# A new front, a shifted block order and a second load of v in an attention and MoE kernel

## The chip, the cores and the metric

The kernel runs on one core of a Trainium2 chip. The metric is the device time of one execution in microseconds (us); lower is better. A profile comes from one profiled execution, and its span runs from the first to the last instruction of that execution.

## The reference

Shapes: q, k, v are `[8, 8, 576, 64]` (batch, head, token, width) in float32; the two weights are `[512, 2048]` and `[2048, 512]`.

```
q_d, k_d, v_d = means over groups of 4 tokens           # 144 coarse tokens
out_d     = softmax(q_d k_d^T / 8) v_d                  # full attention, coarse
out_local = softmax(q k^T / 8 where |i - j| < 4) v      # a band of 7 keys for each query
attn      = repeat(out_d, 4 times along the tokens) + out_local
x   = attn, heads side by side: [4608, 512]
out = elu(x @ w_in) @ w_out                             # [4608, 512], float32
```

## The kernel before

The work falls into two parts. Attention goes by batch (8 of them) and, in a batch, by pairs of heads (j = 0 to 3). The two matrix products go by blocks of 512 tokens (t = 0 to 8). A batch has 576 tokens, so block t needs batch t and, from block 1 on, the end of the batch before it.

**One pair of heads.** `load` brings q as fp16 (a casting DMA of GpSimd's queue) and k, v as fp32 (SP's queue). Queries are cut into 6 blocks of 96 tokens, so each partition gets 12 runs of 256 bytes; k and v have 6 more partitions, filled by small DMAs, for the 3 neighbours on each side. `cast` turns k and v to fp16 on GpSimd. `transposes` multiplies q and k by constant matrices (QI, KI), which gives in one pass the transposed rows and their means over 4, and does the same for v's means with VR (L172); ScalarE and VectorE evict the results (qt, kt, kd, vd). `scores` makes the band's scores (L200) and the coarse scores (L210), ScalarE takes the exponentials (L218, L222), and VectorE multiplies by a 0/1 mask (L228).

**One batch.** `denominators` sums the exponentials of all four pairs by matmuls with an indicator (IND) and VectorE takes the reciprocal. The reciprocals are spread over the partitions: for batch 0 by matmuls (`spread_pe`), for the others through DRAM, by DMAs that ScalarE's queue issues (`spread_out`, `spread_in`). `outputs` makes the weighted sums of v (L321, L327), VectorE multiplies by the reciprocals (gn, ln), and GpSimd adds the two parts into xt, the input of the first product (L348).

**One block.** `mm1(t, fc)`, fc = 0 to 15, is 4 matmuls of 128x512 (L364), an exponential on ScalarE (L369), and two steps on VectorE (L370, L373) that give elu. `mm2(t, i)`, i = 0 to 15, is again 4 matmuls (L384); four such steps make 128 tokens of the output, which ScalarE copies and SP stores. So a block costs 32 groups of 4 matmuls. "Group" means such four matmuls below.

**Order.** Nothing is reordered at run time: every step is an event with a time on an abstract scale, the events are sorted, and each engine gets its instructions in that order. One unit of that scale is one `mm1` and, where there is one, one `mm2`. In the kernel before:

```
def start_of(t):
    return 0 if t == 0 else 16 * (t + 1)
...
at(start_of(t) + s + 0.25, mm1, t, s)
at((16 if t == 0 else start_of(t + 1)) + s + 0.75, mm2, t, s)
```

So all of batch 0's attention comes first, then mm1 of block 0 alone (with batch 1 among it), mm2 of block 0 alone, mm1 of block 1 alone (with batch 2), and from then on mm1 of block t beside mm2 of block t - 1, with batch t + 1 among them. The last two blocks have no attention beside them. "Stage t" means mm1 of block t and what stands beside it.

PSUM has 8 banks: two double banks (tag `two`) for all of attention, two banks `hp` for mm1, two `misc` for mm2, the denominators and half of the early mm1.

Of the kernel before, what the change touches and what calls it, by code (L numbers as in the profile page):

```python
# [9 lines left out]
FP16 = mybir.dt.float16  # L10
FP32 = mybir.dt.float32
AB = mybir.AluOpType
AF = mybir.ActivationFunctionType

# [3 lines left out]
QB, KW, NB = 96, 102, 6  # L18
HB = 3 * QB
QW, KWW = QB + 24, 24 + KW  # L20
DM, DFF, NTOK = 512, 2048, 4608
TBLK = 512
# [3 lines left out]
RW = S + SD  # L26
KG = SD // 2


def _np_consts():  # L30

    off = np.concatenate([np.arange(96), np.arange(-3, 0), np.arange(96, 99)])
    m = np.zeros((KW, NB, QB), dtype=np.float16)
    for c in range(NB):
        for u in range(QB):
            ok = (np.abs(off - u) < 4) & (off + QB * c >= 0) & (off + QB * c < S)
            m[ok, c, u] = 1.0
    r = np.zeros((KW, 24), dtype=np.float16)
    r[np.arange(96), np.arange(96) // 4] = 0.25
    qi = np.concatenate([np.eye(96, dtype=np.float16), r[:96]], axis=1)  # L40
    ki = np.concatenate([r, np.eye(KW, dtype=np.float16)], axis=1)
    vr = np.zeros((KW, 120), dtype=np.float16)
    vr[:, 48:72] = r
    indl = np.zeros((128, 37), dtype=np.float16)
    indl[:, 5] = 1.0
    seed = np.zeros((2, 32 + HB), dtype=np.float16)
    seed[0, 6:32] = 1.0
    seed[1, 4:6] = 1.0
    seed[0, 32:] = 1.0
    seed[1, 32 + SD :] = 1.0  # L50
    sel = np.zeros((NPAIR, 32, 3, 2, 64), dtype=np.float16)
    for e in range(2):
        for g in range(2):
            sel[:, 2 * e + g, g, e] = 1.0
        sel[:, 4 + e, 2, e] = 1.0
    return m, qi, ki, vr, indl, seed, sel.reshape(128, 384)
# [12 lines left out]
def kernel(  # L69
# [11 lines left out]
    ps = ctx.enter_context(tc.tile_pool(name="ps", bufs=1, space=bass.MemoryType.PSUM))  # L81
    dr = ctx.enter_context(tc.tile_pool(name="dr", bufs=1, space=bass.MemoryType.DRAM))
    ctx.enter_context(nc.allow_low_precision("fp16 operands of TensorE"))

    def const(a, name):
        t = sb.tile(list(a.shape), FP16, tag=name, bufs=1, name=name)
        nc.sync.dma_start(out=t[:], in_=nc.inline_tensor(a, name=name + "c").ap())
        return t

    def two(name):  # L90
        return ps.tile([128, 2, 512], FP32, tag="two", bufs=2, name=name)

    m_np, qi_np, ki_np, vr_np, ind_np, seed_np, sel_np = _np_consts()
    QI, KI = const(qi_np, "QI"), const(ki_np, "KI")
    consts = {}

    def late_consts():
        consts["VR"] = const(vr_np, "VR")
        consts["MASK"] = const(m_np, "MASK")
        consts["IND"] = const(ind_np, "IND")  # L100
        consts["SEED"] = const(seed_np, "SEED")
        consts["SEL"] = const(sel_np, "SEL")

    WI = sb.tile([128, DMC, DFF], FP16, tag="WI", bufs=1, name="WI")
    WO = sb.tile([128, FCN, DM], FP16, tag="WO", bufs=1, name="WO")

    def load_weights(i):

        if i < 8:
            src = moe_w_in.rearrange("(c p) m -> p c m", p=128)[:, :, 256 * i : 256 * i + 256]  # L110
            to = WI[:, :, 256 * i : 256 * i + 256]
        else:
            n = 2 * (i - 8)
            src = moe_w_out.rearrange("(c p) m -> p c m", p=128)[:, n : n + 2, :]
            to = WO[:, n : n + 2, :]
        nc.gpsimd.dma_start(out=to, in_=src)


    st16, stT, stB, stS, stR = {}, {}, {}, {}, {}

    st32 = {}

    def load(b, j):
        q16 = sb.tile([QB, 2, NB, 64], FP16, tag="q16", bufs=5, name="q16")
        k32 = sb.tile([KW, 2, NB, 64], FP32, tag="k32", bufs=3, name="k32")
        v32 = sb.tile([KW, 2, NB, 64], FP32, tag="v32", bufs=3, name="v32")

        def rows(src, c0, nblk, tok, n):
            a = src[b, 2 * j]
            blocks = [[QB * D, 2 * NB]] if nblk == NB else [[S * D, 2], [QB * D, nblk]]  # L130
            return bass.AP(
                tensor=a.tensor, offset=a.offset + (QB * c0 + tok) * D,
                ap=[[D, n], *blocks, [1, D]],
            )

        nc.gpsimd.dma_start(out=q16[:], in_=rows(q, 0, NB, 0, QB))  # L136
        for src, dst in ((k, k32), (v, v32)):
            nc.sync.dma_start(out=dst[0:96], in_=rows(src, 0, NB, 0, QB))
            lo = 1 if (b, j) == (0, 0) else 0
            hi = NB - 1 if (b, j) == (B - 1, NPAIR - 1) else NB  # L140
            if lo or hi < NB:
                nc.gpsimd.memset(dst[96:KW, :, 0 if lo else NB - 1, :], 0.0)
            for c0, nblk, tok, p in ((lo, NB - lo, -3, 96), (0, hi, QB, 99)):
                to, a = dst[p : p + 3, :, c0 : c0 + nblk, :], rows(src, c0, nblk, tok, 3)
                if nblk == NB:
                    nc.sync.dma_start(out=to, in_=a)
                else:
                    for e in range(2):
                        nc.sync.dma_start(out=to[:, e], in_=a[:, e])
        st32[(b, j)] = (q16, k32, v32)  # L150

    def cast(b, j):
        q16, k32, v32 = st32.pop((b, j))
        k16 = sb.tile([KW, NB, 2, 64], FP16, tag="k16", bufs=2, name="k16")
        v16 = sb.tile([KW, NB, 2, 64], FP16, tag="v16", bufs=8, name="v16")
        nc.gpsimd.tensor_copy(out=k16[:], in_=k32[:].rearrange("p e c d -> p c e d"))  # L156
        nc.gpsimd.tensor_copy(out=v16[:], in_=v32[:].rearrange("p e c d -> p c e d"))  # L157
        st16[(b, j)] = (q16, k16, v16)


    def transposes(b, j):
        q16, k16, v16 = st16.pop((b, j))
        VR = consts["VR"]
        tq, tk = two("tq"), two("tk")
        for c in range(NB):
            for e in range(2):
                nc.tensor.matmul(  # L167
                    tq[64 * e : 64 * e + 64, c // 3, QW * (c % 3) : QW * (c % 3) + QW],
                    q16[:, e, c, :], QI[:], start=True, stop=True,
                )  # L170
        for c in range(NB):
            nc.tensor.matmul(  # L172
                tq[0:KG, c // 3, 3 * QW : 3 * QW + 128],
                VR[:, 48 - 24 * (c % 3) : 120 - 24 * (c % 3)], v16[:, c, :, :],
                start=(c % 3 == 0), stop=(c % 3 == 2),
            )
        qt = sb.tile([128, 2, 3 * QW], FP16, tag="qt", bufs=2, name="qt")
        nc.scalar.copy(out=qt[:], in_=tq[:, :, 0 : 3 * QW])  # L178
        vd = sb.tile([KG, 2, 128], FP16, tag="vd", bufs=8, name="vd")
        nc.vector.tensor_copy(out=vd[:], in_=tq[0:KG, :, 3 * QW : 3 * QW + 128])  # L180
        for c in range(NB):
            nc.tensor.matmul(  # L182
                tk[:, c // 3, KWW * (c % 3) : KWW * (c % 3) + KWW], k16[:, c, :, :], KI[:],
                start=True, stop=True,
            )
        tk4 = tk[:, :, 0 : 3 * KWW].rearrange("p g (c w) -> p g c w", w=KWW)
        kt = sb.tile([128, 2, 3, KW], FP16, tag="kt", bufs=2, name="kt")
        nc.scalar.copy(out=kt[:], in_=tk4[:, :, :, 24:KWW])  # L188
        kd = sb.tile([128, 2, 3, 24], FP16, tag="kd", bufs=2, name="kd")
        nc.vector.tensor_copy(out=kd[:], in_=tk4[:, :, :, 0:24])  # L190
        stT[(b, j)] = (qt, kt, kd, vd, v16)


    def scores(b, j):
        qt, kt, kd, vd, v16 = stT.pop((b, j))
        sc = [two("sc"), two("sc")]
        for c in range(NB):
            for e in range(2):
                r = slice(64 * e, 64 * e + 64)
                nc.tensor.matmul(  # L200
                    sc[e][0:KW, c // 3, QB * (c % 3) : QB * (c % 3) + QB],
                    kt[r, c // 3, c % 3, :],
                    qt[r, c // 3, QW * (c % 3) : QW * (c % 3) + QB],
                    start=True, stop=True,
                )
        for kg in range(2):
            for e in range(2):
                r = slice(64 * e, 64 * e + 64)
                qd = _free(qt[r, 0, QB : QB + 1], [[QW, NB], [1, 24]])
                nc.tensor.matmul(  # L210
                    sc[e][0:KG, kg, HB : HB + SD],
                    _free(kd[r, 0, 0, 0:1], [[1, SD]])[:, KG * kg : KG * kg + KG], qd,
                    start=True, stop=True,
                )
        pex = sb.tile([KW, 2, S], FP16, tag="pex", bufs=2, name="pex")
# [272 lines left out]
```

## Time and profile before

| | us |
|---|---|
| three runs | 399.96, 401.83, 402.24 (median 401.83) |
| span of the profiled execution | 396.9 |
| first matmul of mm1 (block 0) | 46.40 after the start |
| end of the last mm2 matmul | 392.96 after the start |
| TensorE busy | 354.1 (89% of the span) |
| VectorE busy | 244.8 (62%) |
| ScalarE busy | 203.8 (51%) |
| GpSimd busy | 136.6 (34%) |

The profiled execution's own device time is not given apart from its span. The median of the three runs is 4.9 us above that span, and this 4.9 us is taken as what lies around a span. PE is TensorE, DVE is VectorE, ACT is ScalarE, POOL is GpSimd. In a timeline a row gives the start, the time from the first to the last of the merged instructions, the engine, the line, what is written from what, and in brackets the idle time before it with what ended it.

### The profile page before, as it was taken

Reading aid. Unit: us, or ns where it says so; the run is one execution under the profiler, and the core shown is the slowest. Engines: PE = TensorE matmul, PEld = TensorE weight load, DVE = VectorE, ACT = ScalarE, POOL = GpSimd, SP = SyncE. Lnnn points to the kernel's source line nnn. Section 1 sums busy time; section 2 is a strip of 40 time slices with the busy share of each in tenths; the row PEclk is TensorE's granted clock in tenths of the full one; section 3 lists DMA queues with packets and bytes.
Section 4 is the critical chain, followed back from the end, with each engine's and each line's share of the span. In section 5 each row is a group of like instructions: output and inputs, shape, how many; then the busy total and the mean of one; then the engine's idle time right before and its main releaser. Section 6 shows DMA issues by size and latency. Waiting matters only on the chain.

```text
span 396.9 us, 8379 instructions
## 1 busy us (share of the span) xinstructions
PE 354.1 (89%) x3244; PEld 183.9 (46%) x3244; DVE 244.8 (62%) x460; ACT 203.8 (51%) x377; POOL 136.6 (34%) x184
## 2 busy tenths in 40 slices
PE   0465699996987899999999999999999899999995
PEld 0343344553544455545555554555544444444442
DVE  0123578643697976877697769766977575555510
ACT  1363158643675475657556664666375334444421
POOL 4375694402930860383038204800520040000000
PEclk9999999998998999999999999999999999999999
DMA  9899999728996892997399439906401400101112
GB/s 125 154 187 176 182 191 183 106 25 167 202 125 146 168 85 55 206 196 48 79 229 168 31 96 226 168 2 138 122 26 36 129 28 26 54 26 38 43 53 80
DMA packets 138083, 44.91 MB, mean 113 GB/s; under 512 B 122580, under 2 KB 133436, under 8 KB 138044
## 3 DMA queue, kind: packets, MB, share of 16 engines
q1 hardware_dynamic: 85644, 29.79, 31.9%
q0 software_dynamic: 43776, 8.92, 25.9%
q10 hardware_dynamic: 8624, 5.68, 6.5%
q8 instruction: 25, 0.41, 0.5%
q14 instruction: 14, 0.11, 0.1%
HBM read 43.33 MB, written 9.95 MB: 134 GB/s over the span
## 4 chain that ended last, share of the span: by engine, by line
PE 77%; DVE 6%; ACT 5%; DMA 4%; ACTq 2%; issue 2%; POOL 1%; SPq 1%; POOLq 0%; DVEq 0%
PE op L384 30%; PE hp L364 28%; PE sc L200 4%; PE tq L172 3%; PE tq L167 3%; DMA v<-in_v_dram 3%; PE lg L321 3%; DVE gt L373 2%; ACTq L272 2%; PE tk L182 2%; ACT pex L218 2%; DVE e L370 1%; DMA rd<-rc 1%; DVE mex L228 1%; POOL xt L348 1%
## 5 line engine op out<-in xcount | busy, mean ns | idle before, releaser
L364 PE MATMUL hp<-xt,WI 128*128 128x512 f16 x576 | 150.1, 388 | 2.5 <-POOL xt L348 1.4
L384 PE MATMUL op<-WO,gt 128*128 128x512 f16 x576 | 145.8, 382 | 0.0
L369 ACT ACTIVATE e<-hp 128x512 f16<-128x512 f32 x144 | 85.6, 601 | 106.2 <-PE hp L364 96.3
L373 DVE SCALAR_TENSOR_TENSOR gt<-hp,e 128x512 f16<-128x512 f32 x144 | 99.6, 692 | 5.4
L370 DVE TENSOR_SCALAR e<-e 128x512 f16<-128x512 f16 x144 | 55.9, 388 | 53.1 <-ACT e L369 52.0
L364 PEld LDWEIGHTS <-WI 128*128 128x128 f16 x576 | 54.4, 99 | 68.4 <-issue 9.3
L384 PEld LDWEIGHTS <-gt 128*128 128x128 f16 x576 | 54.4, 98 | 63.5 <-issue 1.8
L156 POOL CAST k<-k 102x768 f16<-102x768 f32 x32 | 26.8, 836 | 95.1 <-DMA k<-in_k_dram 54.0
L348 POOL TENSOR_TENSOR xt<-ln,gn 128x512 f16<-128x512 f16 (+7 forms) x64 | 42.1, 689 | 46.9 <-DVE ln L339 46.9
L218 ACT ACTIVATE pex<-sc 102x576 f16<-102x576 f32 x64 | 41.4, 647 | 21.8 <-PE sc L210 21.6
L228 DVE TENSOR_TENSOR mex<-pex,MASK 102x1152 f16<-102x1152 f16 x32 | 26.2, 817 | 38.6 <-ACT pex L218 38.4
L157 POOL CAST v<-v 102x768 f16<-102x768 f32 x32 | 29.7, 927 | 37.3 <-DMA v<-in_v_dram 37.2
L178 ACT CAST qt<-tq 128x720 f16<-128x720 f32 x32 | 24.3, 758 | 35.3 <-PE tq L172 31.2
L390 ACT COPY os<-op 128x512 f32<-128x512 f32 x36 | 21.2, 588 | 19.9 <-PE op L384 19.9
L200 PE MATMUL sc<-qt,kt 64*102 64x96 f16 x384 | 18.9, 224 | 12.9 <-ACT kt L188 7.2
L180 DVE CAST vd<-tq 72x256 f16<-72x256 f32 x32 | 13.4, 417 | 27.5 <-ACT qt L178 26.5
L136 POOL DMA_DIRECT2D q<-in_q_dram x32 | 28.6, 893 | 3.9 <-DMA WI<-in_moe_w_in_dram 3.0
L167 PE MATMUL tq<-QI,q 96*64 96x120 f16 x384 | 17.4, 230 | 10.4 <-DMA q<-in_q_dram 5.9
L200 PEld LDWEIGHTS <-kt 64*102 64x102 f16 x384 | 14.0, 132 | 27.1 <-ACT kt L188 13.2
L222 ACT ACTIVATE dex<-sc 72x288 f16<-72x288 f32 x64 | 25.8, 404 | 0.0
L172 PE MATMUL tq<-v,VR 102*72 102x128 f16 x192 | 18.0, 234 | 7.0 <-POOL v L157 7.0
L339 DVE TENSOR_TENSOR ln<-lg,rcb 128x576 f16<-128x576 f32 x32 | 23.9, 746 | 0.0
(35 smaller groups left out, 211.9 us busy)
## 6 DMA issues: line engine op xcount, KB each, us to landing
k<-in_k_dram SPq DMA_DIRECT2D x32, 288.0 KB
v<-in_v_dram SPq DMA_DIRECT2D x32, 288.0 KB
out_dram<-os SPq DMA_DIRECT2D x36, 256.0 KB
q<-in_q_dram POOLq DMA_DIRECT2D x32, 144.0 KB, 4.5
rcb<-rd ACTq DMA_DIRECT2D x14, 288.0 KB
WI<-in_moe_w_in_dram POOLq DMA_DIRECT2D x8, 256.0 KB, 10.8
WO<-in_moe_w_out_dram POOLq DMA_DIRECT2D x8, 256.0 KB, 9.3
rcb<-rd ACTq DMA_DIRECT2D x14, 72.0 KB
```

Of the source, the lines that this page charges most:

```text
L157: nc.gpsimd.tensor_copy(out=v16[:], in_=v32[:].rearrange("p e c d -> p c e d"))
L167: nc.tensor.matmul(tq[64 * e : 64 * e + 64, c // 3, QW * (c % 3) : QW * (c % 3) + QW], q16[:, e, c, :], QI[:], start=True, stop=True,)
L172: nc.tensor.matmul(tq[0:KG, c // 3, 3 * QW : 3 * QW + 128], VR[:, 48 - 24 * (c % 3) : 120 - 24 * (c % 3)], v16[:, c, :, :], start=(c % 3 = ...
L200: nc.tensor.matmul(sc[e][0:KW, c // 3, QB * (c % 3) : QB * (c % 3) + QB], kt[r, c // 3, c % 3, :], qt[r, c // 3, QW * (c % 3) : QW * (c % ...
L218: nc.scalar.activation(out=pex[:, e, :].rearrange("p (g u) -> p g u", g=2), in_=sc[e][0:KW, :, 0:HB], func=AF.Exp, scale=SCALE,)
L228: nc.vector.tensor_tensor(out=mex[:], in0=pex[:], in1=mk2, op=AB.mult)
L348: nc.gpsimd.tensor_tensor(out=xt(t)[:, j, t0 - TBLK * t : t1 - TBLK * t], in0=ln[:, a:z], in1=_rep4(gn[:, a // 4 : z // 4]), op=AB.add,)
L364: nc.tensor.matmul(hp[:], WI[:, dc, 128 * fc : 128 * fc + 128], x[:, dc, :], start=(dc == 0), stop=(dc == DMC - 1),)
L369: nc.scalar.activation(out=e[:], in_=hp[:], func=AF.Exp)
L370: nc.vector.tensor_scalar(out=e[:], in0=e[:], scalar1=1.0, scalar2=-1.0, op0=AB.min, op1=AB.add)
L373: nc.vector.scalar_tensor_tensor(out=gts[t][:, fc, :], in0=hp[:], scalar=0.0, op0=AB.max, in1=e[:], op1=AB.add)
L384: nc.tensor.matmul(op_[:], gts[t][:, fc, 128 * tt : 128 * tt + 128], WO[:, fc, :], start=(fc == 0), stop=(fc == FCN - 1),)
```

## The change

In words:

- **Front.** q and k of batches 0 and 1 come as fp16 through GpSimd's queue in runs of 1536 bytes (6 tokens in a row on each of 96 partitions), transposed by TensorE's transpose (into fp16 PSUM) and put in order by the eviction. The sums over 4 tokens are taken from the transposed rows: by VectorE in batch 0, by GpSimd in batch 1. The band's mask is added by a matmul (`masked_scores`) before the exponential, so batches 0 and 1 need no multiplication by the mask. 14 matmuls of zeros run first and 2 more after the first pair. PSUM is split otherwise while batch 0 runs (three double banks, two single ones). The order of batch 0 is written out pair by pair (`first_batch`).
- **Constants** are loaded through ScalarE's queue. The weights come in larger pieces: w_in between the loads of batch 1, w_out within stage 0.
- **Order.** `start_of(t)` is 16 t: mm1 of block 1 runs beside mm2 of block 0. Four of the 16 steps of `mm2(0, i)` come at the end of stage 0.
- **Spreading.** Batches 0 to 2 spread the reciprocals by matmuls (one pair at a time); the others through DRAM as before, but SP's queue issues the DMAs.
- **Later batches.** q of batches 2 to 7 comes as fp32 by SP's queue and is cast by GpSimd; its transposing takes 6 matmuls per pair instead of 12. k has no extra partitions: the neighbours come from a padded transposed row (KT). v has 8 extra rows on each side within one DMA.
- **Sums of v.** Batches 3 to 7 load v a second time (`load_groups`, runs of 1024 bytes), and GpSimd adds the four tokens (`group_v`); the matmuls with VR are gone there.

The core of the diff:

```diff
-QB, KW, NB = 96, 102, 6
+QB, KW, NB, PAD = 96, 112, 6, 8
+RUNS = 2
+VG = 3
...
     def const(a, name):
-        nc.sync.dma_start(out=t[:], in_=nc.inline_tensor(a, name=name + "c").ap())
+        nc.scalar.dma_start(out=t[:], in_=nc.inline_tensor(a, name=name + "c").ap())
...
+    def load_runs(b, j, n, src, name):
+        t = fs.tile([QB, 2 * n, TPP * D], FP16, tag=f"{name}{b}{j}", bufs=1, name=name + "16")
+        nc.gpsimd.dma_start(out=t[:], in_=bass.AP(tensor=a.tensor, offset=a.offset,
+            ap=[[TPP * D, QB], [S * D, 2 * n], [1, TPP * D]]))
...
+    def load_groups(n):
+            g = v4s[(b, j)] = sb.tile([KG, 2, 2, 4 * D], FP32, tag="v4", bufs=2, name="v4")
+            nc.sync.dma_start(out=g[:], in_=bass.AP(tensor=a.tensor, offset=a.offset,
+                ap=[[4 * D, KG], [S * D, 2], [4 * D * KG, 2], [1, 4 * D]]))
...
+    def group_v(b, j):
+        nc.gpsimd.tensor_tensor(out=g[:, :, :, 0 : 2 * D], in0=g[:, :, :, 0 : 2 * D],
+            in1=g[:, :, :, 2 * D :], op=AB.add)
+        nc.gpsimd.tensor_tensor(out=vd[:].rearrange("p (g e d) -> p e g d", g=2, e=2),
+            in0=g[:, :, :, 0:D], in1=g[:, :, :, D : 2 * D], op=AB.add)
...
+    def transposes(b, j):
+                if b < RUNS:
+                    for e in range(2):
+                        nc.tensor.transpose(t[64 * e : 64 * e + 64, 128 * c : 128 * c + QB],
+                            x[:, e, D * c : D * c + D], C["NI"][0:QB, 0:QB])
+                else:
+                    nc.tensor.matmul(t[:, a : a + QW], x[:, c, :, :], C["QI"][:], start=True, stop=True)
...
+    def masked_scores(b, j, e, sc):
+        for g in range(2):
+            nc.tensor.matmul(sc[0:KW, 512 * g : 512 * g + HB], C["NI"][:, 0:KW],
+                C["NI"][:, KW + HB * g : KW + HB * g + HB], start=True, stop=False)
+        for c in range(NB):
+            nc.tensor.matmul(sc[0:KW, a : a + QB], s["kt"][r, QB * c : QB * c + KW],
+                s["qt"][c][r], start=False, stop=c % 3 == 2)
...
     def spread_out(b):
-        nc.scalar.dma_start(out=rd[:], in_=stR[b][:])
+        nc.sync.dma_start(out=rd[:], in_=RC[b][:])
...
+    def keep(t, n, w=512):
+        for _ in range(n):
+            nc.tensor.matmul(t[:, 0:w], Z[:, 0:128], Z[:, 0:w], start=True, stop=True)
+
+    def first():
+        nc.vector.memset(Z[:], 0.0)
+        t = two("sc")
+        keep(t, 14)
+        for name, a in (("NI", ni_np), ("QI", qi_np)):
+            C[name] = const(a, name)
+        for j, n in ((0, 1), (1, 1), (2, 2)):
+            run_pair(0, j, n)
...
+    def then():
+        for j in range(NPAIR):
+            load_v(0, j)
+        cast_v(0, 0)
+        load_wi(0, 256)
+        run_pair(1, 0)
+        cast_v(0, 1)
+        load_wi(256, 512)
...
+        T(0)          # first_batch: transposes, evictions (q on ACT, k on DVE), sums by DVE
+        then()
+        scored(0)     # masked_scores and exponentials of pair 0
+        T(1)
+        coarsed(0)    # coarse scores and exponentials
+        keep(one("junk"), 2)
+        scored(1)
+        T(2)
+        coarsed(1)
+        v_first(b, 0) # VR matmuls for v's sums
+        scored(2)
+        dens((0, 1))  # denominators, reciprocals
+        T(3)
+        coarsed(2)
+        spread(0, dve)
...           (outputs of pair 0, then scores of pair 3, then for each
...            pair: spread, denominators, outputs, gn and ln, xt)
+        spread(3, act)
+        ends(3)
+        load_wi(1024, 1536)
+        cast_v(1, 0)
+        run_pair(1, 3)
+        load_v(1, 3)
+        load_wi(1536, 2048)
...
     def start_of(t):
-        return 0 if t == 0 else 16 * (t + 1)
+        return 16 * t
...
+        if b == 1:
+            base, tr, sc_ = 0, (-0.1, 2.3, 6.3, 10.3), (0.3, 4.3, 8.3, 12.3)
+        elif b == 2:
+            base, tr, sc_ = 16, (0, 3, 6, 9), (1.5, 4.5, 7.5, 10.5)
...
+    for n in range(3):
+        at(11.2 + 2 * n, load, n)      # batch 2's first pairs
+    for n in range(4):
+        at(2 + 2 * n, load_wo, n)
...
-            at((16 if t == 0 else start_of(t + 1)) + s + 0.75, mm2, t, s)
+            at(start_of(t + 1) + (s + 0.75 if t else s - 4 + 0.75 if s > 3 else 0.11 * s - 0.62), mm2, t, s)
```

## The prediction

> **What bounds the kernel now.** I read the windows by stage first, then TensorE's timeline where it idles, then the DMA view of one stage. The stretches are: before mm1, stage 0's mm1, mm2 of block 0, stage 1, and one later stage.
>
> ```profile
> core 0: us, PE busy (x) PEld busy (x) DVE busy (x) ACT busy (x) POOL busy (x), PEclk, DMA share, GB/s
> 0.00:46.40 46.40, 21.30 (x273) 15.98 (x273) 12.06 (x23) 15.36 (x29) 23.09 (x35) 1.00 1.12 163
> 46.40:71.70 25.30, 22.97 (x170) 10.77 (x169) 19.55 (x38) 15.29 (x29) 17.49 (x24) 1.00 1.41 179
> 71.70:103.50 31.80, 27.09 (x326) 14.90 (x325) 13.77 (x26) 14.69 (x29) 11.31 (x17) 0.95 0.64 115
> 103.50:131.60 28.10, 23.57 (x287) 13.14 (x287) 22.81 (x43) 19.01 (x38) 12.27 (x15) 0.94 0.92 151
> ...
> 169.90:208.20 38.30, 38.30 (x390) 19.95 (x389) 28.38 (x54) 23.58 (x44) 15.19 (x20) 1.00 0.76 135
> ```
>
> From 131.6 on TensorE sets the time: a stage with attention takes 38.3 us and TensorE is busy in all of it. Its 32 groups cost 32 x 0.864 = 27.65 us (in the chain of waits each set of four 512-column matmuls takes 0.86 us), so one batch of attention costs TensorE 38.3 - 27.65 = 10.65 us. Ahead of 131.6 it is otherwise: TensorE is busy for less than half of the first 46.4 us and idles 11.5 us of the next 85.2. What it does there is also slow. These are rows of its timeline, for transposes of q (12 matmuls), for the start of mm1 and after an idle stretch:
>
> ```profile
> 23.45 0.81 PE L167 MATMUL tq<-QI,q 96*64 96x120 f16 x12 [1.02 <-ACT dex L222]
> 28.81 0.81 PE L167 MATMUL tq<-QI,q 96*64 96x120 f16 x12 [1.03 <-ACT dex L222]
> ...
> 49.63 7.33 PE L364 MATMUL hp<-xt,WI 128*128 128x512 f16 x21 [0.69 <-POOL xt L348]
> 56.89 0.51 PE L167 MATMUL tq<-QI,q 96*64 96x120 f16 x12
> ...
> 92.35 1.01 PE L200 MATMUL sc<-qt,kt 64*102 64x96 f16 x12 [3.68 <-ACT kt L188]
> 93.53 3.08 PE L384 MATMUL op<-WO,gt 128*128 128x512 f16 x8
> ```
>
> The same 12 matmuls take 0.81 us in the front and 0.51 us at 56.89; pairs follow at 5.36 us, each waiting for the last one's exponentials. A 512-column matmul costs 0.43 us cold (weight loads at 93.94, 94.36, 94.79 and 95.22) and 0.216 warm. 21 matmuls in 7.33 us are then some 5.7 us of cold work ahead of the warm rate, and after a gap of 3.68 us some 3.9 us pass.
>
> Sum for before: 46.4 + 288 groups (248.8) + 7 batches (74.6) + losses = 393.0, so the losses after 46.4 are 23.2 us; then 3.9 us of tail (last copy, last store). 396.9 of span, plus 4.9 to the median of 401.83.
>
> **The front.** Zero matmuls: 14 x 0.43 = 6.0 us, after a memset of about 1 us: TensorE is free at 7.1. Before's first q landed at 5.88 with 1152 runs of 256 bytes; here it is 192 runs per tensor, so q and k of pair 0 are there by about 7, and the zeros hide behind that; if not, they cost up to 2 us. From there I follow the written order at warm rates; the times in this list count from 7.1:
> - Transposes 2 x 0.44; q's eviction 0.64 on ScalarE (576 of 720 elements of a 0.76 row); k's 0.76 on VectorE (row L297). k is there 2.0 after the start.
> - Per further pair, scores 1.1 (8 matmuls, one head at a time), transposes 0.9 and k's eviction with its two waits: 3.0. Pairs 1 and 2: 4.9 and 7.9. With the denominators and first reciprocal between, 4.2 for pair 3: 12.1.
> - Its second score bank is free only when pair 0's reciprocals are copied (14.0), so its exponentials end at 15.4 and the coarse ones at 16.2.
> - The ends: VectorE runs a reciprocal (about 1.0, half of the 1.95 row) and gn, ln (0.30 + 0.75) per pair, ending at 18.9, 21.0 and 22.5; the last xt add (0.6 to 1.06; 0.9 taken) ends at 23.4.
>
> v(0,0) is issued on SP only after a memset that VectorE reaches behind pair 0's sums (10.4); the first v took 6.2 us before, and 4 to 6 are taken, plus 0.93 of GpSimd's cast, where the sums of v are due on TensorE at 14.3: 1 to 3 us late, 1.2 taken. First mm1: 7.1 + 23.4 + 1.2 = **31.7** instead of 46.4. All this needs DMA: q and k of batch 0 (2.4 MB), v (1.4), half of w_in (2.1), three pairs of batch 1 (2.8) are 8.7 MB in 30 us, 290 GB/s read; with casting loads in it, 40 to 50 us moved 1.47 MB written as fp16 (2.9 read) and 0.34, 328 GB/s. So it fits, barely.
>
> **Stage 0.** 16 groups of mm1 and 4 of mm2: 17.3. Batch 1 by warm rows per pair: transposes 0.88, masked scores 1.1, coarse 0.27, sums of v 0.40, denominators 0.45, spread 0.33, outputs 0.42 = 3.85, x 4 = 15.4, less the first transposes (hidden in the front), plus pair (2,0)'s 1.06: 15.6. Sum 32.9. VectorE has 16 x 1.1 + 4 x 1.05 + 5 of others + 2 x 0.9 = 29, ScalarE 26: both under it, close. The sums of q and k of batch 1 stand on GpSimd behind xt, two weight DMAs (0.78), a cast and two more DMAs; pair (1,0)'s coarse scores wait for that, 1 to 3 us, 2.0 taken. End of stage 0: 31.7 + 32.9 + 2.0 = 66.6.
>
> **The rest.** 128 groups of mm1 and 140 of mm2: 231.6. That mm2 of block 0 now lies beside mm1 of block 1 changes no matmul; it only gives less time to fetch batch 2. Batch 2: 10.65 - 1.06 - 0.35 + 2.0 (spread and denominators by smaller matmuls) = 11.2. Batches 3 to 7: the sums of v leave TensorE (6 matmuls, 0.40 per pair, first to first) and q needs 6 matmuls instead of 12 (0.1): 10.65 - 2.05 = 8.6 each, 43.0. Together 285.8. Stage 36.3 instead of 38.3.
>
> What must hide there: GpSimd gets two adds per pair (1.06 + 0.63 by the xt rows of 512 and 256 elements) and a cast of q (0.84) for a DMA issue (0.89): 15.2 becomes 22 of 36.3. VectorE loses vd (4 x 0.42). ScalarE loses 3 us of DMA issue, which SP takes: the spread DMAs now stand behind loads whose buffers GpSimd must free; outputs come 4.8 units (11 us) after `spread_out`, and the first of the two hops took 3.45 us before (84.72 to 88.17), so it hides unless the queue adds some 5 us. DMA, per stage from this view (169.9 to 208.2):
>
> ```profile
> q1 hardware_dynamic: 11003, 3.71, 41.4%
> q0 software_dynamic: 4672, 0.59, 24.4%
> ```
>
> 3.71 MB in 41.4% of 38.3 us is 234 GB/s on this queue. After: q, k 2.36, v 1.38, v again 1.18, out 1.05, spread 0.81 = 6.8 MB, 29 of 36.3 us. It fits on the mean. Stalls: 1.1 us near each of two xt (as before) and 1.0 for batch 2's first loads: 3.2.
>
> Sum: 66.6 + 285.8 + 3.2 + 3.9 = 359.5 of span, + 4.9 = **364 us**: 14.7 from the front, 10.3 from batches 3 to 7, the rest from stalls and cold work at the two early blocks, less the dearer batch 1.
>
> **Rivals.**
> 1. The front stays cold (25%). Its matmuls come in bursts, as before, where TensorE was busy for 5.4 to 6.5 of each 10 us and stayed at 0.81. For warm: gaps of about 1 us here, and at 104 to 122, with a gap of 1.4, rows stayed at 0.51. Cold, some 8 us of the front's 16 that lie on its path double: 364 + 8 = 372. The Trainium skill (TensorE: Matmul & The Clock Gate, Part 4: PE-mode transpose) says that a transpose in TensorE's own mode does not count as busy for the clock; batches 0 and 1 now use that mode, before did not, so no row shows it, and by that rule this is the likelier case.
> 2. Loads are late (17%): w_out, the rest of w_in and batch 2 all fall into stage 0, after a front that ran at the limit; 10 to 20 us gave 154 GB/s. With 8 to 14 us lost at T(1), v or pair (2,0): 375.
> 3. VectorE bounds the later stages (8%). The windows of line L370 alone (elu's first step) show 0.41 us each beside GpSimd's work and 0.30 where GpSimd rests:
>
> ```profile
> 131.60:323.00 191.40, 33.91 (x82) 1.00 0.60 112
> 323.00:378.30 55.30, 9.46 (x32) 1.00 0.10 39
> ```
>
> GpSimd gets half as much again, which by these rows adds 0.05 to each, 0.8 us per stage, to a VectorE that is at 28.4 of 38.3 and loses 1.7; but it comes in bursts, and two `hp` banks hide little. If stages stay at 38.3: 364 + 5 x 2 = 374.
> 4. Slower (4%): the second load of v makes DMA the pace. At 154 GB/s a stage takes 6.8 / 0.154 = 44 us, 7.8 more in six stages: 364 + 47 = 411. It decides from 158 GB/s (43 us per stage). Against it: 234.
> 5. The shift does nothing: stage 1 waits for batch 2 as long as before's stage 1 (4.5 us idle): 364 + 4 = 368, inside the main case.
>
> **Numbers.** Main case 46%: 364, own range 352 (no stalls, data in time) to 371. Range **350 to 385**: it leaves out the far part of case 2, case 4 and unknown gains, some 15%. A difference of 0.5% (2 us) is about what can be told from no change: faster 0.95, same 0.01, slower 0.04.
>
> **What would show it.** Right: first mm1 at 29 to 35, transposes of the front at 0.5 us per 12, later stages at 36.3 with TensorE busy throughout. Wrong: rows at 0.8 in the front (case 1), TensorE waiting for casts at the start of stage 1 (case 2), `hp` waiting for VectorE's gt (case 3), gn or transposes waiting for DMA in each stage (case 4).

## The result, and the profile after

The changed kernel takes 404.15 us (median of 7 runs, 403.55 to 407.98) where the kernel before took 401.07 on the same chip: a ratio of 1.0104, 95% interval 1.0065 to 1.0143. It is slower by 1%; 364 was forecast, with 0.95 for faster. The profiled execution has a span of 402.7 us (396.9 before). The page of after, busy time by engine, TensorE's clock in 40 slices, and the chain that ended last:

```profile
PE 369.8 (92%) x3244; PEld 194.6 (48%) x3244; DVE 270.3 (67%) x461; ACT 206.9 (51%) x386; POOL 174.4 (43%) x225
...
PEclk9555799989989689999999999999999999999999
...
PE 64%; DVE 18%; ACT 5%; POOL 4%; DMA 4%; issue 3%; SPq 0%; DVEq 0%; ACTq 0%; POOLq 0%
```

TensorE is busy more of the span than before, yet less of the chain is its own: VectorE has 18% of it (6% before). The clock is at half in the second to fourth slice and drops again near 84, 111, 133 and 145 us. The windows between the starts of mm1 of blocks 0 to 4 answer to those of before:

```profile
core 0: us, PE busy (x) PEld busy (x) DVE busy (x) ACT busy (x) POOL busy (x), PEclk, DMA share, GB/s
0.00:41.40 41.40, 36.06 (x400) 24.97 (x401) 18.30 (x36) 15.57 (x30) 18.45 (x31) 0.63 0.85 143
41.40:84.53 43.13, 37.93 (x436) 22.15 (x435) 27.53 (x58) 22.95 (x44) 24.53 (x38) 0.94 1.08 161
84.53:134.66 50.13, 43.19 (x449) 23.43 (x447) 31.19 (x60) 30.51 (x59) 24.73 (x31) 0.91 0.91 171
134.66:179.54 44.88, 40.38 (x353) 20.34 (x352) 35.96 (x52) 24.80 (x47) 25.30 (x31) 0.94 0.76 153
179.54:218.32 38.78, 36.55 (x341) 18.81 (x340) 33.65 (x49) 23.83 (x45) 22.47 (x27) 1.00 0.81 167
```

TensorE fills 36 of the first 41.4 us, at a mean clock of 0.63. (The 1.00 that the prediction's windows give for the front of the kernel before is no measurement: the clock's records in that trace begin at 55.0 us, and its rows of 0.81 us there are cold ones.) In the last row its work has shrunk as forecast (36.55 for 38.30 before), but the stage is longer than before's 38.3; VectorE has gone from 28.38 to 33.65 us and GpSimd from 15.19 to 22.47. TensorE's timeline, at places like those shown of before:

```profile
5.63 0.45 PE L263 MATMUL tq<-NI,q 96*64 96x96 f16 x12
...
13.87 0.69 PE L263 MATMUL tq<-NI,q 96*64 96x96 f16 x12
...
82.40 0.78 PE L269 MATMUL tq<-QI,q 96*128 96x120 f16 x6 [3.00 <-POOL q L183]
```

The same 12 transposes go from 0.45 to 0.69 us inside the front, and ahead of batch 2 TensorE stands 3.0 us for one cast of q on GpSimd. In the DMA view of 179.54 to 218.32 the main queue moves 6.42 MB:

```profile
q1 hardware_dynamic: 17225, 6.42, 80.3%
```

No wait of TensorE in that stretch ends on a transfer. Where the time stands, from the starts of mm1 (the predicted column from the prediction's terms: stage 1 is 27.65 + 11.2, the last row holds its 3.2 of stalls and the tail):

| us | predicted | after | sums of v on TensorE | casts on ScalarE |
|---|---|---|---|---|
| first mm1 | 31.7 | 41.4 | 41.8 | 39.8 |
| stage 0 | 34.9 | 43.1 | 42.9 | 41.3 |
| stage 1 | 38.9 | 50.1 | 50.7 | 52.5 |
| stage 2 | 36.3 | 44.9 | 42.7 | 43.4 |
| stages 3 to 5 | 108.9 | 116.8 | 114.9 | 111.5 |
| rest | 108.8 | 106.4 | 106.2 | 106.5 |
| span | 359.5 | 402.7 | 399.2 | 395.0 |

The last two columns are experiments below. Every kernel below is compared with the kernel before on its own chip (397.7 to 398.8 us there), so ratios are what to compare, with after's 1.0104.

### The profile page after: what moved, and what is told of

Read it like the earlier page. It is cut to its first block, busy times and chain, and to the rows that moved or that the text cites. A ratio compares the mean times of both kernels' runs of the same rounds, so it can differ in the third digit from the quotient of the medians.

```text
span 402.7 us, 8286 instructions
## 1 busy us (share of the span) xinstructions
PE 369.8 (92%) x3244; PEld 194.6 (48%) x3244; DVE 270.3 (67%) x461; ACT 206.9 (51%) x386; POOL 174.4 (43%) x225
## 4 chain that ended last, share of the span: by engine, by line
PE 64%; DVE 18%; ACT 5%; POOL 4%; DMA 4%; issue 3%; SPq 0%; DVEq 0%; ACTq 0%; POOLq 0%
PE hp L545 24%; PE op L565 23%; DVE e L551 9%; DVE gt L554 4%; DVE ln L520 3%; PE sc L351 2%; ACT e L550 2%; POOL xt L529 2%; DMA k<-in_k_dram 2%; PE tk L269 1%; PE sc L340 1%; PE lg L501 1%; DVE mex L387 1%; DMA rd<-rc 1%; PE sc L361 1%
## 5 line engine op out<-in xcount | busy, mean ns | idle before, releaser
L551 DVE TENSOR_SCALAR e<-e 128x512 f16<-128x512 f16 x144 | 80.1, 556 | 54.6 <-ACT e L550 53.7
L529 POOL TENSOR_TENSOR xt<-ln,gn 128x64 f16<-128x64 f16 (+7 forms) x61 | 40.6, 693 | 131.3 <-DVE ln L520 131.3
L372 ACT ACTIVATE pex<-sc 112x576 f16<-112x576 f32 x64 | 41.4, 647 | 29.6 <-PE sc L361 19.9
L387 DVE TENSOR_TENSOR mex<-pex,MASK 112x1152 f16<-112x1152 f16 x24 | 24.7, 1030 | 14.6 <-ACT pex L372 14.6
L230 POOL CAST v<-v 112x768 f16<-112x768 f32 x32 | 27.2, 850 | 10.0 <-DMA v<-in_v_dram 10.0
L237 POOL TENSOR_TENSOR v<-v 72x512 f32<-72x512 f32 x20 | 27.9, 1394 | 1.9 <-DMA v<-in_v_dram 1.8
L283 ACT CAST qt<-tq 128x720 f16<-128x720 f32 x24 | 18.1, 756 | 18.5 <-PE tq L324 11.2
L183 POOL CAST k<-k 96x768 f16<-96x768 f32 x24 | 19.9, 831 | 1.4 <-DMA k<-in_k_dram 1.4
L183 POOL CAST q<-q 96x768 f16<-96x768 f32 x24 | 19.9, 829 | 1.0 <-PE tq L269 1.0
L351 PE MATMUL sc<-qt,kt 64*112 64x96 f16 x288 | 13.8, 221 | 6.4 <-DVE kd L315 4.0
L241 POOL TENSOR_TENSOR vd<-v 72x256 f16<-72x256 f32 x20 | 18.9, 943 | 1.6
```

What stands on the lines that cost most here:

```text
L183: nc.gpsimd.tensor_copy(out=x[:], in_=t[:].rearrange("p (e c) d -> p c e d", e=2))
L237: nc.gpsimd.tensor_tensor(out=g[:, :, :, 0 : 2 * D], in0=g[:, :, :, 0 : 2 * D], in1=g[:, :, :, 2 * D :], op=AB.add,)
L351: nc.tensor.matmul(sc[e][0:KW, a : a + QB], s["kt"][r, QB * c : QB * c + KW], s["qt"][c][r], start=True, stop=True,)
L372: nc.scalar.activation(out=h2(s["pex"][:, e, :]), in_=g2(sc[0:KW], 0, HB), func=AF.Exp, scale=SCALE)
L387: nc.vector.tensor_tensor(out=s["mex"][:], in0=s["pex"][:], in1=mk2, op=AB.mult)
L529: eng.tensor_tensor(out=xt(t)[:, j, t0 - TBLK * t : t1 - TBLK * t], in0=ln[:, a:z], in1=_rep4(gn[:, a // 4 : z // 4]), op=AB.add,)
```

## The experiments

**Theory.** Two causes. In the later stages VectorE is held up by GpSimd, more than in proportion to GpSimd's extra work. In the front the clock falls to half. Rivals: the second load of v, the shift of blocks, a front bound by its chain of waits, VectorE simply too busy.

What suggested the first cause is elu's first step as a group, before and then after (busy us, then mean ns):

```profile
L370 DVE TENSOR_SCALAR e<-e 128x512 f16<-128x512 f16 x144 | 55.9, 388 | 53.1 <-ACT e L369 52.0
```

```profile
L551 DVE TENSOR_SCALAR e<-e 128x512 f16<-128x512 f16 x144 | 80.1, 556 | 54.6 <-ACT e L550 53.7
```

and VectorE's timeline at the start of stage 2, with GpSimd's beside it:

```profile
136.04 0.28 DVE L551 TENSOR_SCALAR e<-e 128x512 f16<-128x512 f16 x1
...
137.24 4.43 DVE L551 TENSOR_SCALAR e<-e 128x512 f16<-128x512 f16 x1 [0.20 <-ACT e L550]
```

```profile
136.85 0.82 POOL L183 CAST q<-q 96x768 f16<-96x768 f32 x1
137.61 0.82 POOL L183 CAST k<-k 96x768 f16<-96x768 f32 x1
...
140.70 0.82 POOL L230 CAST v<-v 112x768 f16<-112x768 f32 x1
```

An instruction of 0.28 us takes 4.43: it begins inside a train (instructions back to back) of six casts of 0.82 and ends as the train ends, 0.18 us into the add of v that follows. TensorE waited 2.43 us for a step that stood behind it on VectorE (kd), up to 142.66, and from 143.8 to 147.2 us the clock was at half. Adds into xt can hold the step as well: four in a row held it for 2.53 us at 215.01. The trains form because GpSimd runs in order: it waits for VectorE's ln at an add into xt (20.38 us before 128.31) and then runs all the casts that have come due. In the kernel before GpSimd's casts were interrupted by the issues of q's casting loads, and no first step of elu took over 1.17 us.

**e1: sums of v on TensorE again**

```
-VG = 3
+VG = 8
```

> All sums of v go back to TensorE (no second load of v, no GpSimd adds; 20 pairs get 6 matmuls, about 0.34 us each, 1.4 us per stage). Theory A (GpSimd's back-to-back work holds up VectorE's elu step): the longest elu first step falls from 4.4 to about 2.5 us (casts of q, k, v still come in one run), stages 3 to 5 stay near 38 us, stages 1 and 2 get some 5 us shorter, total 394 to 400 us. Rival B (the extra DMA makes loads late): the elu steps stay as they are and the gain shows as fewer waits for loads, total about 400. If neither matters: 404 + 7 = 411 us.

Measured: 1.0073 (1.0034 to 1.0112), elu's first step 417 ns on the mean over the kernel instead of 556, stage 2 42.7, stages 3 to 5 38.8, 37.4 and 38.7. Three of these four stages are shorter than after's, stage 3 is as long (38.8), although TensorE does 1.4 us more in each. The longest step did not fall to 2.5 us: behind four adds into xt and a cast it took 3.30 us, once in stage 3 and once in stage 5, and stage 4, where none took over 1.26, is the short one. Stage 1 (50.7) did not get shorter.

**e2: q of batches 2 to 7 by casting DMA**

```
-        nc.sync.dma_start(out=t[:], ...)                # q: FP32, cast by GpSimd
+        nc.gpsimd.dma_start(out=t[:], ...)              # q: FP16, 12 matmuls as in batch 0
```

> q of batches 2 to 7 comes by a casting DMA from GpSimd's queue as in the kernel before (12 transposing matmuls per pair, 0.1 us more), so GpSimd loses one cast of 0.83 us per pair; the second load of v and the adds stay. Theory A: runs on GpSimd get shorter, elu's first step falls from a mean of 0.74 to about 0.5 us in stages 3 to 5, which take 37 to 38 instead of 38.9 us; total 392 to 399. Rival B (DMA): the casting load takes more DMA time per byte than the plain one, so no gain or a loss: 404 to 410 us.

Measured: 1.0181 (1.0105 to 1.0258), no gain. Issuing such a load occupies GpSimd for 0.90 us, as long as the cast did, so GpSimd was not relieved, and TensorE got six matmuls more per pair. The first step fell only from 0.74 to 0.68 in stages 3 to 5. In the trace five of the longer holds end where a DMA issue begins (k's cast, v's cast, issue): there the issue let VectorE through and the cast ahead of it had not. Once, at 138.78, it did not: the step stood for 3.31 us through an issue and a cast more, and got in between that cast and the next.

**e3: two zero matmuls ahead of each score tile of batch 0**

```
+                keep(SC[j][e], 2)
                 masked_scores(b, j, e, SC[j][e])
```

> Two 512-column matmuls of zeros ahead of each of the 8 masked score tiles of batch 0 (16 matmuls, 3.5 us at the full clock, 6.9 at half). Theory C (the clock at half rate from 10.7 to 44.8 us is what delays the front): the clock stays at 1.0, the transposes at 0.45 us per 12, first mm1 at 33 to 36 us instead of 41.4; total 397 to 400. Rival D (waits for data, evictions and VectorE set the front): first mm1 stays at 40 to 43 us, total 403 to 406. If the clock falls all the same: first mm1 at 44 to 47, total 407 to 410.

Measured: 1.0145 (1.0053 to 1.0237), no gain that the runs can tell. First mm1 in the profile 38.7 instead of 41.4, with the clock at full until 22.1 us and at half for most of the time to 42.6.

**e4: which matmuls hold the clock**

```
+        for i in range(240):
+            nc.tensor.transpose(tt[...], Z[0:96, 0:64], I)
+        keep(t, 20)
+        for i in range(240):
+            nc.tensor.matmul(pp[...], Z[0:96, 0:64], I, start=True, stop=True)
+        keep(t, 20)
```

> The clock by itself: after the first loads are issued, 240 transposes of 96 columns in TensorE's transpose mode back to back, 20 matmuls of 512 columns, 240 plain matmuls with the same operands and sizes back to back, 20 of 512 columns; the rest as in the changed kernel. If transposes do not count as work for the clock (the page's rule), rows of the transposes go from about 0.04 to 0.08 us apart after 3.4 to 6.8 us, and the plain ones stay at the full rate. Rival: small matmuls of either kind do not count, and both trains fall; or both count, and neither falls, which leaves the gaps in the front as the cause. The total grows by some 30 to 45 us.

Measured (one run, 432.5 us), as windows over the transposes, the plain matmuls, the front's first 7 us, the 3.4 us after that, and the next 6.9 (columns as above; the clock is the third from last):

```profile
6.40:16.70 10.30, 10.30 (x242) 10.23 (x241) 0.00 (x0) 0.00 (x0) 0.00 (x0) 1.00 0.55 85
21.10:31.40 10.30, 10.30 (x241) 10.25 (x240) 0.00 (x0) 0.00 (x0) 0.00 (x0) 1.00 0.01 3
35.90:42.90 7.00, 6.28 (x115) 4.55 (x114) 4.93 (x8) 4.49 (x9) 0.00 (x0) 1.00 0.24 54
42.90:46.30 3.40, 1.78 (x21) 1.25 (x20) 2.36 (x4) 1.36 (x4) 2.45 (x4) 1.00 1.11 217
46.30:53.20 6.90, 6.17 (x97) 4.92 (x98) 3.44 (x5) 2.82 (x6) 6.66 (x10) 0.50 1.36 209
```

Ten us of nothing but transposes leave the clock at full, as plain matmuls of the same size do. It falls after a window of 3.4 us of which TensorE filled 1.78, waiting 1.62 for the first v. The Trainium skill (TensorE: Matmul & The Clock Gate, Part 4: PE-mode transpose) says that transposes do not count as busy for the clock; here they held it for three windows, so that rule is not what cooled the front. (Whether they can raise a cold clock no run here shows.)

**e5: the clock held at full through the front**, by 50 zero matmuls

```
+                keep(SC[j][e], 3)          # also 2 ahead of den, 2 ahead of rb, 3 ahead of lg
                 masked_scores(b, j, e, SC[j][e])
```

> The changed kernel, with more zero matmuls of 512 columns in the front: three ahead of each of the eight masked score tiles of batch 0, two ahead of each denominator and each spread, three ahead of each output tile. Theory (the clock falls to half when TensorE is covered for less than about 0.6 of a window of 3.41 us, and the small matmuls of the front do not bring it back): the clock record stays full from about 4 us on, rows of 12 transposes stay at 0.45, and the first mm1 comes at 34 to 37 instead of 41.4; total 4 to 7 us below the changed kernel. Rival (the front is a chain of waits on ScalarE and VectorE, and the clock matters little): first mm1 at 38.5 to 41, as with two zeros ahead of the scores (38.74), or later, since some 10 us of zeros are added.

Measured: 1.0215 (1.0178 to 1.0253). The clock stayed at full from about 6 to 46.9 us, and still the first mm1 came at 41.7. First the front of after, then that of e5, as windows of most of it (from pair 2 on and from pair 1 on):

```profile
14.10:38.90 24.80, 23.30 (x276) 17.52 (x272) 11.06 (x18) 10.16 (x22) 12.76 (x19) 0.50 0.89 149
```

```profile
10.10:39.70 29.60, 27.54 (x369) 16.33 (x366) 13.39 (x22) 12.60 (x27) 12.99 (x19) 1.00 0.90 153
```

TensorE is all but full in both. By the starts in the timeline the 50 zeros take 12.0 us; without them the same rows would come to 41.7 - 12.0 = 29.7 us, an estimate that takes it that no wait comes in their place. So the work at full clock is near what was forecast (31.7), but these 50 matmuls cost as much as the clock gives. The expected 34 to 37 was missed. The rival (a chain of waits on ScalarE and VectorE) is not what fills the 41 us: TensorE is all but full, and e3's front took 38.7. That such a chain would bound a full-clock front without zeros is not ruled out.

**e6: elu's two VectorE steps in another form**

```
-        nc.vector.tensor_scalar(out=e, in0=e, scalar1=1.0, scalar2=-1.0, op0=min, op1=add)
-        nc.vector.scalar_tensor_tensor(out=gt, in0=hp, scalar=0.0, op0=max, in1=e, op1=add)
+        ...                                    # r has one buffer; e has two here, three in after
+        nc.vector.tensor_scalar(out=r, in0=hp, scalar1=0.0, scalar2=-1.0, op0=max, op1=add)
+        nc.vector.scalar_tensor_tensor(out=gt, in0=e, scalar=1.0, op0=min, in1=r, op1=add)
```

> The changed kernel with the two VectorE steps of elu written differently: first r = max(hp, 0) - 1, from PSUM, then gt = min(e, 1) + r, a step with two tensor inputs; in place of e = min(e, 1) - 1 from SBUF to SBUF, then gt = max(hp, 0) + e. GpSimd's work is untouched. Theory (GpSimd's trains hold up only the SBUF-to-SBUF step in VectorE's fast form): both steps take 0.6 to 0.7 us with nothing over 1, TensorE's waits for gt (4.3 to 4.8 us in stages 3 to 5) go, and these stages take 37.0 to 37.6 instead of 38.6 to 39.4, stage 2 42 or less; total 6 to 14 us below the changed kernel although VectorE is no less busy. Rival (GpSimd slows every VectorE access to SBUF, or VectorE is simply too busy): one of the two steps shows means over 0.8 and single ones over 2 us, stages 3 to 5 stay at 38.6 or go above 39.

Measured: 1.0800 (1.0752 to 1.0849). The theory's form was wrong. Groups of VectorE, after first and then e6 (mean ns last but for the idle time):

```profile
L554 DVE SCALAR_TENSOR_TENSOR gt<-hp,e 128x512 f16<-128x512 f32 x144 | 99.6, 692 | 5.4
L551 DVE TENSOR_SCALAR e<-e 128x512 f16<-128x512 f16 x144 | 80.1, 556 | 54.6 <-ACT e L550 53.7
```

```profile
L555 DVE SCALAR_TENSOR_TENSOR gt<-e,r 128x512 f16<-128x512 f16 x144 | 139.4, 968 | 5.3
L552 DVE TENSOR_SCALAR r<-hp 128x512 f16<-128x512 f32 x144 | 98.7, 686 | 32.2 <-ACT e L550 28.0
```

The step that reads PSUM keeps its 0.69 us beside any train, in both kernels. The one with both inputs in SBUF, 0.69 alone, is held as the short step was (2.54 and 2.80 us in stage 3). What counts in these two forms is where the operands lie. The Trainium skill (SBUF — State Buffer, Who interferes with whom) states it so: GpSimd shares one pair of VectorE's ports to SBUF, and a VectorE instruction in a two-port mode, or with two inputs in SBUF beside a GpSimd instruction that reads SBUF, excludes and is excluded by that instruction; with one SBUF input or none outside those modes it is free. The 692 and 686 beside 968 and 556 agree. Stages 3 to 5 took 43.5, 43.4 and 42.6 us, so longer holds went with longer stages. This run does not prove the dose by itself: with e's two buffers ScalarE's exponential waited 17.9 us for gt (2.8 in after), which can lengthen stages too.

**e7: the second load of v without the adds**

```
-VG = 3
+VG = 8                                             # load_groups still issued for batches 3 to 7, unused
```

> Sums of v on TensorE for all batches, as in the run with sums on TensorE (ratio 1.0073 to the kernel before), but the second load of v is issued as in the changed kernel and not used. It shows the transfers without GpSimd's adds. Theory (the loss lies in GpSimd's work): stages 2 to 5 as without the load, 42.7, 38.8, 37.4, 38.7, ratio 1.005 to 1.010. Rival (the second load makes DMA or SP's queue the limit): stages 2 to 5 0.5 us or more longer each, gn or transposes waiting for DMA, ratio 1.013 or above.

Measured: 1.0071 (1.0049 to 1.0093), as e1's 1.0073. The transfer costs nothing that the runs can tell. What the adds cost is not clear from these totals, since the intervals of e1, e7 and after (1.0065 to 1.0143) overlap; GpSimd's part shows in e10.

**e8: without the shift of blocks**

```
-        return 16 * t
+        return 0 if t == 0 else 16 * (t + 1)       # mm2 of block 0 then stands alone, batch 2 over 32 slots
```

> The changed kernel without the shift of blocks: mm1 of block 1 starts after mm2 of block 0, as in the kernel before, and batch 2's attention is spread over the 32 slots of mm2 of block 0 and mm1 of block 1 one after the other. Same work, other order. Theory (the shift makes stage 1 dense but puts batch 2's chain in a single row, where normalise, spread and scores wait for VectorE): the start of mm1 of block 2 moves from 134.7 to 129 to 132, total 2 to 5 us lower. Rival (the shift is neutral, the losses come from half clock and GpSimd): start of block 2 within 1.5 us of 134.7, total within 2 us. If the shift was worth what it was meant for, block 2 starts 2 to 4 us later.

Measured: 1.0242 (1.0181 to 1.0304), block 2 at 137.4 instead of 134.7 although the front was 1.1 us earlier. Of the outcomes named the last holds: the shift, with batch 2's order that goes with it, is a gain, and the change would have been slower without it.

**e9: 24 zeros instead of 50**

```
+                keep(SC[j][e], 2 if j == 0 else 1)  # also 4 or 1 ahead of vs, 1 ahead of rb and lg
```

> The changed kernel with 24 zero matmuls in the front instead of the 48 of the run that held the clock: two ahead of each score tile of pair 0 and one ahead of those of pairs 1 to 3, four ahead of the first sums of v (where TensorE waited 1.0 to 2.1 us for v), one ahead of the other sums, spreads and three of the output tiles. Theory (a warm front is worth some 12 us of TensorE time, and the zeros that hold the clock cost it back, 0.22 us each): if the clock stays full, first mm1 at 35 to 37.5 and 3 to 5 us off the total; if it falls, 38.5 to 40. Rival (the front's chain on ScalarE and VectorE sets 41 whatever TensorE does): first mm1 at 41 to 42 as with 48 zeros.

Measured (the run that held the clock had 50 zeros, not 48): 1.0033 (0.9995 to 1.0071). Its profiled execution took 405.65 us, 5.9 over its median, so no stage is read from it. The gain over after is some 0.7%, with intervals that just touch.

**e10: casts of q and k of batches 2 to 7 on ScalarE**

```
-            nc.gpsimd.tensor_copy(out=x[:], in_=t[:]...)
+            nc.scalar.copy(out=x[:], in_=t[:]...)
```

> The changed kernel with the casts of q and k of batches 2 to 7 on ScalarE instead of GpSimd (two per pair, 1.6 us of GpSimd's time per pair). Adds, second load and order are untouched. Theory (VectorE's steps from SBUF to SBUF wait for GpSimd's trains): trains are at most three or four long, the first step of elu falls from 0.74 to 0.5 or less in stages 3 to 5 and in stage 2 from 0.88 to below 0.6, stages 3 to 5 take 36.8 to 37.8, stage 2 42 or less; total 5 to 10 us below the changed kernel. Rival (the stages are bound by something else, as the run with q cast by DMA suggests): stages 3 to 5 stay at 38.6 or more, or ScalarE, which gets 6 to 7 us per stage more, becomes late and its exponentials are waited for.

Measured: 0.9956 (0.9918 to 0.9993), 1.5% below after. Windows of stages 2 to 5:

```profile
133.66:177.01 43.35, 40.34 (x353) 20.40 (x352) 31.86 (x52) 31.00 (x57) 20.22 (x24) 0.93 0.79 158
177.01:213.90 36.89, 36.46 (x341) 18.74 (x340) 27.61 (x50) 27.92 (x52) 12.90 (x18) 1.00 0.79 177
213.90:251.98 38.08, 36.69 (x342) 18.75 (x341) 28.67 (x50) 28.83 (x53) 16.91 (x21) 1.00 0.86 180
251.98:288.49 36.51, 36.18 (x342) 18.70 (x341) 28.74 (x50) 28.61 (x53) 17.14 (x22) 1.00 0.59 136
```

VectorE is back at 28 us, elu's first step at 0.46 in stages 3 to 5 (longest 1.37, was 3.00), and two of the three later stages are within 0.6 us of the forecast 36.3, with TensorE all but full. VectorE's instructions are those of after, so what fell is the time they were held, not its work. ScalarE takes 5 us more per stage and nobody waits for it there. This settles most of stages 3 to 5: 111.5 instead of 116.8, for 108.9 forecast. Stage 2 came only to 43.4, against 42 or less expected, although its steps fell to 0.50.

**e11: the adds into xt on VectorE**

```
-            eng = nc.vector if b < 2 and b == t and j >= 3 - b else nc.gpsimd
+            eng = nc.vector if b >= 2 or (b == t and j >= 3 - b) else nc.gpsimd
```

> The changed kernel with the adds into xt of batches 2 to 7 on VectorE instead of GpSimd (four to eight per stage, about 3 us). It takes away the place where GpSimd waits for VectorE and behind which its casts pile up. Theory (long trains come from that wait): the longest first step of elu falls from 4.4 to under 3, its mean in stages 2 to 5 from 0.74 to 0.88 to below 0.65, stages 3 to 5 take 37.3 to 38.3 although VectorE has 3 us more. Rival (GpSimd's sum of work counts, not where it stands): mean of elu's first step 0.7 or more, stages as long as or longer than 38.6.

Measured: 1.0242 (1.0167 to 1.0318). The longest hold fell to 2.55 us, as expected of shorter trains, but the mean in stages 2 to 4 came only to 0.68 to 0.72 (0.61 in stage 5) where below 0.65 was expected, and the adds were now VectorE's own work. So no gain came of shorter trains; how much the added work on VectorE hid, the run does not tell.

**e12, e13, e14: combinations.** e12 is e10 with e9's zeros; e13 is e10 with

```
-            ... s - 4 + 0.75 if s > 3 ...
+            ... 1.3 * (s - 4) + 0.75 if s > 3 ...
```

for mm2 of block 0; e14 has all three.

> Casts of q and k on ScalarE (ratio 0.9956 to the kernel before) together with the 24 zero matmuls in the front (ratio 1.0033 against 1.0104 without). Theory (two separate causes): the gains add, ratio 0.985 to 0.993. Rival (the front is not worth anything once the later stages run freely, or the zeros' gain was the clock's chance): ratio 0.994 to 0.998.

> Casts of q and k on ScalarE, and the twelve groups of mm2 of block 0 that lie in stage 1 spread over all of it (every 1.3 units instead of every unit), so that the last four units, in which batch 2 goes from denominators to xt, have mm2 to cover them. Theory (stage 1 is long because that chain has nothing beside it: 6.8 us of waits, and the half clock that follows each): waits for ln in 120 to 133 us fall from about 3.5 to under 1.5, the half rate windows after them go, stage 1 falls from 52.5 to 47 to 50, total 2 to 5 us lower. Rival (the chain itself sets the time: mm2 moved there delays the matmuls of the chain): stage 1 52 to 54, no gain.

> All three: casts on ScalarE, mm2 of block 0 spread over stage 1, 24 zeros in the front. If the three causes are separate their gains add: ratio 0.978 to 0.988. If stage 1's chain sets the time, as with the casts and the zeros alone.

Measured: e12 0.9906 (0.9871 to 0.9941), e13 1.0019 (0.9979 to 1.0059), e14 0.9909 (0.9878 to 0.9940). e12 beats both kernels: 0.9% under the kernel before, 2% under the change. The zeros gain some 0.5% over e10, with overlapping intervals, and 1.1% over e13, with intervals apart. The clock goes with it: the mean granted clock is 0.96 to 0.99 in e14's ten runs and 0.94 to 0.96 in e13's. The profiled executions of e12 and e14 lie 3.5 and 3.8 us above their medians, and their first mm1 (41.9 and 40.4 us) does not show the gain. Spreading mm2 brings nothing. Stages 0, 1 and 2 of e13:

```profile
41.34:82.67 41.33, 37.41 (x436) 21.64 (x435) 27.54 (x58) 25.88 (x48) 22.86 (x36) 0.95 1.09 174
82.67:135.03 52.36, 42.80 (x451) 23.44 (x448) 31.12 (x60) 37.08 (x69) 15.42 (x20) 0.93 0.82 154
135.03:175.68 40.65, 37.34 (x353) 19.35 (x352) 29.14 (x51) 29.91 (x55) 17.31 (x22) 1.00 0.85 175
```

Stage 1 keeps its 52.4 us with TensorE idle for 9.6 of them. From 99 us on its chain of waits goes hand over hand through TensorE, ScalarE and VectorE (spread, copies of rcb, transposes, gn, ln, scores), each step waiting for the one that empties a `two` tile; from 84.9 to 96.9 us it lies on transfers of v, which after's chain does not have. That this chain sets stage 1 is argued from those rows and from mm2's indifference; no run shortened it.

## Why the prediction was wrong, point by point

The span came out 43.2 us over the sum; the kernel's median lies only 1.45 above its span, where 4.9 were taken.

- **Front, 9.7 us.** The step that failed is "from there I follow the written order at warm rates". They held to 10.7 us; from there to 44.8 the clock was at half. This is rival 1, which had 25% and 8 us. Transposes alone did not do it (e4); the fall at 10.7 came after a window with waits of 0.47, 0.60 and 0.23 us among small matmuls, and whether the waits alone are enough no run separates. The sum of the front at full clock was near (an estimate of 29.7 from e5), but the 50 zeros that held the clock cost 12 us; 24 zeros gained 0.5 to 1.1% of the whole time. v's wait was rightly placed: 1.0 to 2.1 us in e1 and e7, none in after, where TensorE came late itself.
- **Stage 0, 8.2 us over.** Waits of TensorE add up to 5.0 (0.61, 0.44, 0.28, 0.72, 3.00) where 2.0 were taken. They were taken for the sums of q and k on GpSimd, which cost 0.61; the 3.0 is the cast of pair (2,0)'s q, queued behind xt on GpSimd, which the prediction did not cost. Without it (e10) the stage took 41.3. Half clock at both ends costs some 3.0. At full clock the work is 35.1 instead of 32.9, mainly the masked scores: 1.56 us per pair (0.34 for the mask and 0.44 for the scores, per head), not 1.1.
- **Stage 1, 11.2 over.** TensorE idles 6.9 us (the longest 1.73, 1.23 and 0.91, all ending on VectorE or ScalarE) and works at half clock from 109.7 to 113.1 and from 130.2 on, some 2.9 us by the same rows at both rates. The prediction had 3.2 us of stalls for all that follows stage 0, and took this stage's work for a sum of TensorE's, with no chain.
- **Stages 2 to 5, 8.6 and 7.9 over.** In stages 3 to 5 TensorE's saving was right (36.55 busy for 36.3 in stage 3). "Adds 0.05 to each, 0.8 us per stage" was the failed term: elu's first step averaged 0.88 in stage 2 and 0.74 after it, for 0.47 and 0.41 before, 5 to 7 us of VectorE's time per stage. The linear reading of 0.41 against 0.30 missed that a step can wait for the end of a train, and that the change replaced the DMA issues between GpSimd's casts by more casts. This is rival 3, at 8%, in a stronger form. It explains stages 3 to 5 (e10). Of stage 2 it explains less: there e10 took off 1.5 us. Another part is the clock, at half for 5.8 us of stage 2 in after and in e10 and not at all in e13, whose stage 2 took 40.7 us for e10's 43.4: the 2.7 between them is about what 5.8 us at half rate cost. The rest of stage 2 is open.
- **The other rivals.** DMA's pace (4): no, by e7. Late loads (2): DMA has 4% of the chain, as before. The shift doing nothing (5): no, it gains (e8).
- **The chances.** Rivals 1 and 3 were taken as exclusive; both came, together with waits that were not listed. Their prices together, 364 + 8 + 10 = 382, would still lie inside the range. Measured, the front and stages 2 to 5 took 26.2 us over the sum, and stages 0 and 1 another 19.4, for which rivals 1 and 3 had no price.
- **Open:** what would shorten stages 0 and 1 (41.3 and 51.1 us even in e12) beyond clock and GpSimd, and why waits of the same length (2.1 us for ln in e10's stage 2, 2.0 in e13's) bring the clock down in one kernel and not in the other.

## What to carry to other kernels

Work moved to GpSimd is not hidden work when VectorE has SBUF-to-SBUF steps on the path: read the longest single instructions of VectorE beside GpSimd's timeline, not means, and look what separates GpSimd's instructions. ScalarE, with room, was the better place for the casts. A front of small matmuls with gaps should be summed at the cold rate unless the zeros that hold the clock are in the sum too; few of them (24) paid here, 50 did not.

## What the runs showed of the hardware

- VectorE's instruction from SBUF to SBUF stood 4.43 us behind six GpSimd casts in a row: it did not get in between two of them. Not every train does this: in the kernel before, at 205.55 and 210.03 us, a step beside four adds into xt in a row was done 0.15 us after the second (0.76 and 0.75 us in all), where after's step at 215.01 stood until the fourth was over; and in e1, at 178.48, a step got in between two casts (1.37 us). What makes the difference no run shows. The profile counts that time as VectorE's busy time (80.1 us for after's first step of elu, 55.9 before).
- The clock changed in steps of 3.41 us. In the 16 traces, the falls at the end of a run left aside, 65 of 76 came after such a window with TensorE covered for 0.62 or less, and the lowest cover that kept the clock was 0.49 (0.44 at the very end of e4). The other 11 had 0.66 to 0.78, all in fronts of small matmuls; in e5's front three windows of 0.68 to 0.79, with 512-column matmuls in them, kept it. So cover alone does not decide. (Cover is worked out as the share of the window that matmul rows overlap.) The Trainium skill (TensorE: Matmul & The Clock Gate, Part 1) has the same window, but speaks of idle ones for the fall; here half-covered windows were enough.
- At half rate, four windows wholly covered by matmuls of at most 288 columns did not bring the clock back in after's front (between 17.5 and 38.0 us); the first window with mm1's 512-column matmuls did (41.4 to 44.8).
